# Attention with decay and a gated MLP on one core: four temporaries for the conversions of w_out, the first conversion ahead of the first MLP's second stage

## The chip, the cores and the metric

The kernel runs on one core of one Trainium2 chip. The metric is the device time of one execution in microseconds, lower is better. An execution under the hardware profiler gives the trace; its engines are called PE (TensorE, the matrix unit), DVE (VectorE), ACT (ScalarE), POOL (GpSimd) and SP (the queue that starts most transfers).

## The reference

The input is q, k, v for 8 batches, 8 heads, 576 tokens and head dimension 64, with a decay factor f per token. The attention's output, 512 wide, goes into a gated MLP:

```python
scores = scale * np.matmul(q, k.transpose(0, 1, 3, 2))
cum = np.cumsum(np.log(np.clip(f, 0.0001, 1.0)), axis=-1)
scores = np.where(causal, -1e9, scores + cum[:, :, :, None] - cum[:, :, None, :])
attn = softmax(scores);  x = heads_side_by_side(attn @ v)     # (8, 576, 512)
h = np.maximum(x @ w_in, 0.0)                                 # w_in: 512 x 1024
u, v = h[..., :512], h[..., 512:]
v_n = (v - mean(v)) / np.sqrt(var(v) + 1e-06)
v_s = einsum('ts,bsd->btd', w_spatial, v_n) + b_spatial[None, :, None]
return (u * v_s) @ w_out                                      # w_out: 512 x 512
```

Everything is float32.

## The kernel before

**Precision.** TensorE multiplies a rounded 32-bit type at full rate, so that each float32 operand is split into a rounded part (`hi`, tiles with an h or index 0) and the rest (`lo`, an l or index 1), and each product takes three matmuls. w_in and w_out come into the kernel as 64-bit floating-point words. `conv64` (L154) makes one 128-row part of such a matrix into the two 32-bit parts. For a part of 128 × 512 it issues nine operations: ACT takes the magnitude into a temporary called `wa` (L162); DVE runs L163, L165, L166, L168 and L169 (limit, shift and mask, join with the sign, exponent, scale of the low word), where L166 writes into the raw tile and L168 reads it; POOL adds (L171); ACT rounds to the high part (L172); POOL subtracts for the low part (L173). All read or write `wa`, so that a second conversion with the same temporary can begin only when L173 of the one before is done. The parts of w_out are `wo[0]` to `wo[3]`; in the listings they are `wo_` with a number.

**Attention.** `attention(b)` handles the batch's eight heads as four pairs P: scores (tiles `sc` from `ta` and `tb`), on DVE the maximum (L345), on ACT the exponential (L347), on POOL the scaling (L355; the last tokens' tile `tl` in L375 and L378), on TensorE the transposes (`tp`, L401), on ACT and DVE the split of these (`eh` L390, `el` L391), on TensorE the products with `vt`, and on ACT and DVE the split of their result (`xh` L449, `xl` L450). `lo` (L280) splits the next pair's q and k, `vt` (L322) its v, both on POOL.

**The MLP.** `moe(b)` has three stages. In the first, five blocks of `vx` = relu(x·w_in, second half) are normalised (L538 to L555) and split into `vnh` and `vnl`; the fifth block has 64 tokens and keeps both parts in one `vnh` tile (L553). In the second, eight `u` tiles come from the first half of w_in (L559 to L570). In the third, for the first 256 and then the other 320 tokens, four gate tiles are the products of `vnh`, `vnl` with w_spatial (`sph`, `spl`; for the fifth block `spta`) times u, split into `gh`, `gl` (L592, L593), and `w_out_tile` (L605) multiplies 128 of their tokens with the four parts of w_out. The last 64 tokens of two batches share one output tile; their gated parts are kept in the tile `gt`, which the even batch allocates. All of these sums go through two PSUM banks (pool `ps_m`, tile name `ps`), in turn.

**What sets the order.** Both are Python generators. The loop at the end advances attention of the next batch and the MLP of this one in shares of time (`LEAD`, `t_attn`, `t_moe`), and the tile framework's scheduler then orders each engine's instructions, by data, by free buffers and by the marks that `after` sets. A mark such as ("exp", 5, 1, 0) is an exponential of pair 5, head 1, tile 0. `load_late` is a third generator, which reads the late parts of the weights and converts them: it stops at each yielded mark and goes on as soon as attention has reached it (`converted`). At "m2" it waits for `open_m2`, which the first MLP calls ahead of its second stage; this closes the pool `wu` and opens `m2` in its place, for u, the gates, `gt` and the output tile `o`. The parts of w_out are converted after this, at the marks of four steps of pairs 5 and 6, all with the one temporary `o`, which the output tiles use too; the fourth part is read from memory at the first of these marks.

Of the kernel before, what the change touches and what calls it, by code (L numbers as in the profile page):

```python
# [9 lines left out]
F32R = mybir.dt.float32r  # L10
BF16 = mybir.dt.bfloat16
U32 = mybir.dt.uint32
# [14 lines left out]
DM = 512  # L27
# [6 lines left out]
def f32(ap):  # L34
    return ap.bitcast(F32)
# [3 lines left out]
def attn_gmlp_kernel(ctx: ExitStack, tc: tile.TileContext, qk, v, f, w_in, w_sp, b_sp, w_out, out):  # L39
# [9 lines left out]
    NJ = DM // 128  # L49
# [85 lines left out]
    win, wo, raws = {}, {}, {}  # L135
# [15 lines left out]
        raws[tag] = cst.tile([128, DM, 2], U32, name="w64", tag=tag)  # L151
        after(SY.dma_start(out=raws[tag], in_=src), mark)

    def conv64(tag, pool, behind, temp=None):  # L154

        raw = raws.pop(tag)
        lo, hi = raw[..., 0], raw[..., 1]
        a = pool.tile([128, DM], U32, name="wa", tag=temp or "wa")
        w = hi if temp else pool.tile([128, DM], U32, name="w32")[:]
        wf, af = w.bitcast(F32), a[:].bitcast(F32)  # L160

        after(A.activation(af, hi.bitcast(F32), AF.Abs), behind)  # L162
        V.tensor_scalar(out=af, in0=af, scalar1=2.0 ** -15, scalar2=None, op0=ALU.max)  # L163

        V.tensor_scalar(out=a, in0=a, scalar1=3, scalar2=0x3FFFFFF8, op0=ALU.logical_shift_left, op1=ALU.bitwise_and)  # L165
        V.scalar_tensor_tensor(out=w, in0=hi, scalar=0xC0000000, in1=a, op0=ALU.bitwise_and, op1=ALU.bitwise_or)  # L166

        V.tensor_scalar(out=a, in0=w, scalar1=0xFF800000, scalar2=None, op0=ALU.bitwise_and)  # L168
        V.scalar_tensor_tensor(out=af, in0=lo, scalar=2.0 ** -52, in1=af, op0=ALU.mult, op1=ALU.mult)  # L169
        t = cst.tile([128, 2, DM], F32R, name=tag, tag=tag)  # L170
        G.tensor_tensor(out=af, in0=wf, in1=af, op=ALU.add)  # L171
        A.copy(t[:, 0, :], af)  # L172
        G.tensor_tensor(out=t[:, 1, :], in0=af, in1=f32(t[:, 0, :]), op=ALU.subtract)  # L173
        return t
# [10 lines left out]
    def read_out(n, mark):  # L185
        read64(f"wo{n}", wo_v[:, n, :, :], mark)
# [44 lines left out]
    def load_late(wu):  # L231

        br = wu.tile([1, S], F32, name="br", bufs=1)
        bs = [wu.tile([1, S], F32R, name=f"bs{r}", bufs=1) for r in range(2)]
        SY.dma_start(out=br, in_=b_sp)
        yield ("exp", 5, 0, 0)
        read_out(1, ("exp", 5, 0, 0))
        read_out(2, ("exp", 5, 0, 0))
        unit(7, wu, ("exp", 5, 0, 0))
        A.copy(bs[0][:], br)  # L240
        V.tensor_tensor(out=bs[1][:], in0=br, in1=f32(bs[0][:]), op=ALU.subtract)
        for r in range(2):
            SY.dma_start(out=f32(sptb[64 + r:65 + r, :]), in_=f32(bs[r][:]))
        yield "m2"
        for n in range(NJ):
            m = ("exp",) + ((5, 1, 0), (6, 0, 0), (6, 0, 3), (6, 1, 0))[n]
            yield m
            if n == 0:
                read_out(3, m)
            wo[n] = conv64(f"wo{n}", m2[0], m, "o")  # L250
        yield None

    tl = cst.tile([128, 640], F32, name="tl")
# [249 lines left out]
    gt = {}  # L503
# [9 lines left out]
    def moe(b):  # L513
        X = [xs.pop(b * PPB + p) for p in range(PPB)]
        vh, vl = [], []
        for i in range(NB + 1):
            ps = acc(b)
            n = 0
            for p in range(PPB):
                xh, xl = X[p]  # L520
                if i < NB:
                    t = slice(128 * i, 128 * i + 128)
                    terms = ((xh[:, t], 0), (xh[:, t], 1), (xl[:, t], 0))
                else:
                    terms = ((xh[:, TL:640], 0), (xh[:, TL:640], 1))
                for l, r in terms:
                    mm(ps, l, win[p][:, r, :], n == 0, n == len(terms) * PPB - 1)
                    n += 1
                yield 648
            th = mo.tile([128, DM], F32R, name="vnh", tag="vnh", bufs=5)  # L530
            tlo = mo.tile([128, DM], F32R, name="vnl", tag="vnl", bufs=4) if i < NB else None
            x = mo.tile([128, DM], F32, name="vx", tag="vx", bufs=2)
            st = mo.tile([128, 6], F32, name="st", tag="st", bufs=2)
            mv = mo.tile([128, 2], F32, name="mv", tag="mv", bufs=2)
            m = slice(0, 128)
            if i == NB:
                m = slice(0, 64)
                A.copy(x[64:128, :], ps[64:128, :])  # L538
                V.tensor_tensor(out=x[m, :], in0=ps[m, :], in1=x[64:128, :], op=ALU.add)
            A.activation(x[m, :], ps if i < NB else x[m, :], AF.Relu)  # L540
            V.bn_stats(out=st[m, :], in_=x[m, :])
            V.bn_aggr(out=mv[m, :], in_=st[m, :])
            G.tensor_tensor(out=mv[m, 1:2], in0=mv[m, 1:2], in1=lnc[m, 0:1], op=ALU.add)
            G.tensor_tensor(out=mv[m, 1:2], in0=mv[m, 1:2], in1=lnc[m, 1:2], op=ALU.pow)
            V.tensor_scalar(out=x[m, :], in0=x[m, :], scalar1=mv[m, 0:1], scalar2=mv[m, 1:2],  # L545
                            op0=ALU.subtract, op1=ALU.mult)
            A.copy(th[m, :], x[m, :])
            if i < NB:
                G.tensor_tensor(out=tlo, in0=x, in1=f32(th[:]), op=ALU.subtract)
                vl.append(tlo)  # L550
            else:
                A.copy(vb_[m, :], x[m, :])
                G.tensor_tensor(out=th[64:128, :], in0=x[m, :], in1=f32(th[m, :]), op=ALU.subtract)  # L553
            vh.append(th)
            yield 0  # L555
        if b == 0:
            open_m2()
        us = {}
        for j in range(NJ):  # L559
            for t0, nt in HALVES:  # L560
                ps = acc(b)
                n = 0
                for p in range(PPB):
                    xh, xl = X[p]
                    for l, r in ((0, xh), (1, xh), (0, xl)):
                        mm(ps[:, 0:nt], win[NJ + j][:, l, 128 * p:128 * p + 128], r[:, t0:t0 + nt], n == 0, n == 3 * PPB - 1)
                        n += 1
                    yield 369
                us[j, t0] = m2[0].tile([128, 320], F32, name="u", tag="U", bufs=9)
                A.activation(us[j, t0][:, 0:nt], ps[:, 0:nt], AF.Relu)  # L570
        if b % 2 == 0:
            gt[0] = m2[0].tile([128, 2, NJ, 128], F32R, name="gt", tag="gt")
        r0 = 64 * (b % 2)
        for t0, nt in HALVES:
            gh, gl = [], []
            for j in range(NJ):
                ps = acc(b)
                o = ps[:, 0:nt]
                js = slice(128 * j, 128 * j + 128)
                for c in range(NB):  # L580
                    mm(o, vh[c][:, js], sph[c][:, t0:t0 + nt], c == 0, False)
                    mm(o, vh[c][:, js], spl[c][:, t0:t0 + nt], False, False)
                    mm(o, vl[c][:, js], sph[c][:, t0:t0 + nt], False, False)
                    yield 370
                mm(o, vh[NB][:, js], spta[:, t0:t0 + nt], False, False)
                mm(o, vb_[:, js], sptb[:, t0:t0 + nt], False, True)
                yield 246
                g = us[j, t0][:, 0:nt]
                V.tensor_tensor(out=g, in0=o, in1=g, op=ALU.mult)
                gh.append(m2[0].tile([128, 320], F32R, name="gh", tag="GH", bufs=3))  # L590
                gl.append(m2[0].tile([128, 320], F32R, name="gl", tag="U", bufs=9))
                A.copy(gh[j][:, 0:256], g[:, 0:256])  # L592
                G.tensor_tensor(out=gl[j][:, 0:256], in0=g[:, 0:256], in1=f32(gh[j][:, 0:256]), op=ALU.subtract)  # L593
                if t0:
                    th, tlo = (gt[0][:, r, j, r0:r0 + 64] for r in range(2))
                    A.copy(th, g[:, 256:320])
                    G.tensor_tensor(out=tlo, in0=g[:, 256:320], in1=f32(th), op=ALU.subtract)
            for c0 in (0, 128):
                yield from w_out_tile(b, [g[:, c0:c0 + 128] for g in gh], [g[:, c0:c0 + 128] for g in gl],
                                      [(b, t0 + c0, 0, 128)])  # L600
        if b % 2 == 1:
            yield from w_out_tile(b, *[[gt[0][:, r, j, :] for j in range(NJ)] for r in range(2)],
                                  [(b - 1, TL, 0, 64), (b, TL, 64, 64)])

    def w_out_tile(b, ghi, glo, dst):  # L605
# [25 lines left out]
    with tc.tile_pool(name="ws", bufs=2) as ws, tc.tile_pool(name="p0s", bufs=3, space=PSUM) as p0s, \  # L631
            tc.tile_pool(name="p0t", bufs=3, space=PSUM) as p0t:
        PS['s'], PS['t'] = p0s, p0t
        wgen = load_first(ws)
        need = next(wgen)
        for _ in attention(0, ws):
            while need in last:
                need = next(wgen, None)
# [7 lines left out]
    late, m2 = ExitStack(), []  # L646
    wgen = load_late(late.enter_context(tc.tile_pool(name="wu", bufs=1, reuse_waits="tile")))
    need = [next(wgen)]
# [66 lines left out]
```

## Time and profile before

| | us |
|---|---|
| median of 3 runs | 799.14 (799.07 to 799.27) |
| the profiled execution's own time | 797.53 |
| span of its trace | 795.7 |
| mean granted TensorE clock | 0.993 of full |
| PE busy | 778.9 (98%) |
| DVE busy | 556.6 (70%) |
| ACT busy | 534.9 (67%) |
| POOL busy | 476.4 (60%) |

All times in the trace are microseconds from the span's start. A row of the timeline gives the start, the duration, the engine, the line, the operation, the output tile <- the input tiles and the shapes, and in brackets how long the engine had idled and what ended that. A window gives each engine's busy time and number of instructions in a stretch, and the clock that TensorE was granted in it (1.00 is full). The program starts with attention alone; the first MLP runs from about 75 us, and the conversions of w_out lie between 107 and 164 us.

### The profile page before, as it was taken

What the parts mean: (1) busy time and instruction counts of PE and PEld (TensorE: products, weight loads), DVE (VectorE), ACT (ScalarE), POOL (GpSimd) and SP (SyncE); (2) the same over time, 40 slices, a digit from 0 to 9 for tenths busy, and PEclk for the clock granted to TensorE, in tenths of its full rate; (3) what the DMA queues carried; (4) which work ended last, traced back from release to release, by engine and by line L of the source; (5) the groups of instructions that cost most, each with busy time, mean ns of one, the idle gap of its engine ahead of it and who ended that gap; (6) DMA issues with size and microseconds to landing.
All of it is one profiled execution on the core that took longest, in us unless ns stands there. A gap on an engine that the chain in (4) does not pass through costs nothing.

```text
span 795.7 us, 15502 instructions
## 1 busy us (share of the span) xinstructions
PE 778.9 (98%) x4980; PEld 702.3 (88%) x4981; DVE 556.6 (70%) x1665; ACT 534.9 (67%) x1418; POOL 476.4 (60%) x660
## 2 busy tenths in 40 slices
PE   8999989899999999999999999999999999999997
PEld 4767779798999989998999989999899988998996
DVE  7889778975767667766866668766787658674421
ACT  7787678675777777667766668766686767764431
POOL 5777798664865647465655647554776537643251
PEclk9999999999999999999999999999999999999999
DMA  9967744566454565365454555564555465320001
GB/s 246 239 185 185 188 119 121 119 168 171 103 123 119 153 152 142 102 148 136 104 143 129 133 145 114 131 170 135 141 134 138 108 164 134 78 75 14 28 1 67
DMA packets 41713, 103.48 MB, mean 130 GB/s; under 512 B 6831, under 2 KB 8879, under 8 KB 41568
## 3 DMA queue, kind: packets, MB, share of 16 engines
q1 hardware_dynamic: 41306, 101.96, 49.7%
q8 instruction: 40, 0.66, 0.4%
q10 hardware_dynamic: 326, 0.53, 0.3%
q14 instruction: 41, 0.34, 0.1%
HBM read 39.42 MB, written 10.68 MB: 63 GB/s over the span
## 4 chain that ended last, share of the span: by engine, by line
PE 86%; DVE 6%; ACT 3%; POOL 2%; issue 2%; DMA 1%; ACTq 0%; POOLq 0%; DVEq 0%
PE ps L260 45%; PE sc L260 16%; PE x L260 12%; PE tp L401 8%; PE tp L260 2%; PE tp L414 2%; DVE tt L345 1%; POOL tt L355 1%; DVE el L391 1%; DVE xl L450 1%; DVE wa L163 0%; ACT eh L390 0%; DVE vx L545 0%; ACT tt L347 0%; ACT hi L278 0%
## 5 line engine op out<-in xcount | busy, mean ns | idle before, releaser
L355 POOL TENSOR_SCALAR tt<-tt,sm 128x128 f32<-128x128 f32 (+3 forms) x256 | 142.0, 573 | 74.9 <-DVE sm L351 56.4
L345 DVE CUSTOM_DVE_ANT_0 tt<-sc,zm 128x128 f32<-128x128 f32 (+3 forms) x256 | 122.8, 486 | 85.0 <-PE tp L401 63.4
L390 ACT CAST eh<-tp 128x512 fp32r<-128x512 f32 (+1 forms) x270 | 111.4, 426 | 75.4 <-PE tp L401 50.2
L347 ACT ACTIVATE tt<-tt,nm 128x128 f32<-128x128 f32 (+3 forms) x256 | 144.4, 565 | 23.7 <-DVE nm L345 21.9
L391 DVE TENSOR_TENSOR el<-tp,eh 128x512 fp32r<-128x512 f32 (+1 forms) x270 | 127.2, 485 | 26.2 <-ACT eh L390 23.8
L401 PE MATMUL tp<-ident,tt 128*128 128x128 f32 x640 | 111.6, 277 | 4.1 <-DVE el L391 4.1
L260 PE MATMUL sc<-ta 128*128 128x128 f32 (+1 forms) x336 | 109.1, 330 | 2.5 <-DVE nm L345 2.0
L260 PE MATMUL sc<-tb 68*128 68x128 f32 (+1 forms) x336 | 106.2, 320 | 0.0
L260 PE MATMUL x<-eh,vt 128*128 128x320 f32 (+4 forms) x378 | 102.5, 287 | 0.0
L593 POOL TENSOR_TENSOR gl<-u,gh 128x256 fp32r<-128x256 f32 x64 | 47.7, 745 | 87.7 <-ACT gh L592 78.1
L260 PE MATMUL ps<-xh,win 128*128 128x256 f32 (+1 forms) x464 | 99.3, 304 | 0.4 <-ACT u L570 0.3
L280 POOL TENSOR_TENSOR lo<-raw,hi 128x640 fp32r<-128x640 f32 (+1 forms) x56 | 84.2, 1525 | 16.1 <-ACT hi L278 15.9
L260 PE MATMUL ps<-win,xh 128*128 128x512 f32 x296 | 90.6, 396 | 0.0
L260 PE MATMUL x<-el,vt 128*128 128x256 f32 x324 | 90.1, 303 | 0.0
L401 PEld LDWEIGHTS tp<-ident,tt 128*128 128x128 f32 x640 | 76.3, 141 | 14.2 <-issue 2.7
L449 ACT CAST xh<-x 64x256 fp32r<-64x256 f32 (+1 forms) x128 | 49.8, 394 | 42.3 <-PE x L260 40.3
L260 PEld LDWEIGHTS ps<-xh,win 128*128 128x128 f32 x464 | 76.3, 192 | 2.0 <-ACT u L570 0.9
L260 PE MATMUL ps<-sph,vnh 128*128 128x256 f32 (+1 forms) x240 | 73.2, 305 | 0.4 <-ACT o L618 0.4
L260 PEld LDWEIGHTS x<-eh,vt 128*128 128x128 f32 x378 | 71.3, 190 | 2.5 <-POOL vt L322 0.3
L260 PE MATMUL ps<-wo,gh 128*128 128x512 f32 x224 | 71.9, 405 | 0.0
L260 PEld LDWEIGHTS sc<-ta 128*128 128x128 f32 x336 | 64.3, 191 | 8.6 <-DVE nm L345 4.5
L260 PE MATMUL ps<-sph,vnl 128*128 128x256 f32 (+1 forms) x240 | 71.6, 298 | 0.0
(178 smaller groups left out, 1916.4 us busy)
## 6 DMA issues: line engine op xcount, KB each, us to landing
raw<-in_dram SPq DMA_DIRECT2D x28, 608.0 KB
ta<-hi SPq DMA_DIRECT2D x56, 304.0 KB
vraw<-in_dram SPq DMA_DIRECT2D x32, 320.0 KB
tb<-hi SPq DMA_DIRECT2D x56, 160.0 KB
ta<-lo SPq DMA_DIRECT2D x56, 160.0 KB
out_dram<-o SPq DMA_DIRECT2D x32, 256.0 KB
ta<-hi SPq DMA_DIRECT2D x56, 144.0 KB
tb<-lo SPq DMA_DIRECT2D x56, 144.0 KB
```

What stands on the lines that cost most here:

```text
L260: last['mm'] = T.matmul(o, l, r, start=st, stop=sp)
L280: G.tensor_tensor(out=lo[:, c], in0=raw[:, c], in1=f32(hi[:, c]), op=ALU.subtract)
L345: V.tensor_tensor_reduce(out=t, in0=sc[:, 0:n], in1=zm[:, 640 - n:640], scale=-0.125, scalar=3.0e38, op0=ALU.add, op1=ALU.min, accum_out=n ...
L347: last["exp"] = last["exp", P, h, i] = A.activation(t, t, AF.Exp, bias=nm[:, i:i + 1], scale=-1.0, accum_out=se[:, i, 0:1])
L355: G.tensor_scalar(out=t, in0=t, scalar1=sm[:, i:i + 1], scalar2=1.0, op0=ALU.mult, op1=ALU.mult)
L390: A.copy(h_ap, ps)
L391: V.tensor_tensor(out=l_ap, in0=ps, in1=f32(h_ap), op=ALU.subtract)
L401: T.transpose(out=tp[:, (i - c) * 128:(i - c + 1) * 128], in_=tt[h][:, TOFF[i] + 128 * c:TOFF[i] + 128 * c + 128], identity=ident)
L414: T.transpose(out=tp[:, j * 128:(j + 1) * 128], in_=tl[:, c * 128:(c + 1) * 128], identity=ident)
L449: last[P, h] = A.copy(hi, ps[m0:m0 + 64, 0:n])
L450: V.tensor_tensor(out=lo, in0=ps[m0:m0 + 64, 0:n], in1=f32(hi), op=ALU.subtract)
L593: G.tensor_tensor(out=gl[j][:, 0:256], in0=g[:, 0:256], in1=f32(gh[j][:, 0:256]), op=ALU.subtract)
```

## The change

The four conversions no longer share one temporary. The first part is converted while the pool `wu` is still open, with that pool's temporary `wb` and ahead of "m2", at the mark ("exp", 5, 0, 2), and the read of the fourth part moves to this mark too. The second and third use the two buffers of a tag `gt`, the fourth uses `o`. The gate tile `gt`, until now one tile for both parts, becomes two tiles with the same tag, allocated when the second group of tokens begins; before that, the generator of conversions is run to its end. So all conversions stand in the program ahead of the first w_out tile that could want a buffer of theirs. The marks of the second to the fourth part are (5,1,0), (6,0,0) and (6,0,3). No operation is added or removed.

```diff
-    def conv64(tag, pool, behind, temp=None):
+    def conv64(tag, pool, behind, temp=None, bufs=None):
...
-        a = pool.tile([128, DM], U32, name="wa", tag=temp or "wa")
+        a = pool.tile([128, DM], U32, name="wa", tag=temp or "wa", bufs=bufs)
...
+        yield ("exp", 5, 0, 2)
+        read_out(3, ("exp", 5, 0, 2))
+        wo[0] = conv64("wo0", wu, ("exp", 5, 0, 2), "wb")
         yield "m2"
-        for n in range(NJ):
-            m = ("exp",) + ((5, 1, 0), (6, 0, 0), (6, 0, 3), (6, 1, 0))[n]
+        for n, m, tag, bufs in ((1, (5, 1, 0), "gt", 2), (2, (6, 0, 0), "gt", 2), (3, (6, 0, 3), "o", 1)):
+            m = ("exp",) + m
             yield m
-            if n == 0:
-                read_out(3, m)
-            wo[n] = conv64(f"wo{n}", m2[0], m, "o")
+            wo[n] = conv64(f"wo{n}", m2[0], m, tag, bufs)
         yield None
...
-        if b % 2 == 0:
-            gt[0] = m2[0].tile([128, 2, NJ, 128], F32R, name="gt", tag="gt")
         r0 = 64 * (b % 2)
         for t0, nt in HALVES:
+            if t0 and b % 2 == 0:
+                while need[0]:
+                    need[0] = next(wgen)
+                gt[0] = [m2[0].tile([128, NJ, 128], F32R, name="gt", tag="gt", bufs=2) for r in range(2)]
...
-                    th, tlo = (gt[0][:, r, j, r0:r0 + 64] for r in range(2))
+                    th, tlo = (gt[0][r][:, j, r0:r0 + 64] for r in range(2))
...
-            yield from w_out_tile(b, *[[gt[0][:, r, j, :] for j in range(NJ)] for r in range(2)],
+            yield from w_out_tile(b, *[[gt[0][r][:, j, :] for j in range(NJ)] for r in range(2)],
```

Lines from `load_late` on shift by one, from the gate stage on by three. What the scheduler makes of the change is seen in three places.

DVE, where the second part's conversion begins. A row is the line, the operation and out<-in; `w_1051`, `w_1053` and `w_1081` are the raw second, third and fourth part. Before:

```order
L163 TENSOR_SCALAR wa<-wa 128x512
L545 TENSOR_SCALAR vx<-vx,mv 64x512
L391 TENSOR_TENSOR el<-tp,eh 128x128
L165 TENSOR_SCALAR wa<-wa 128x512
L350 TENSOR_REDUCE sm<-se_108 128x4
L166 SCALAR_TENSOR_TENSOR w_1051<-w_1051,wa 128x512
L351 RECIPROCAL sm<-sm 128x4
L345 ISA tt_67,nm<-sc,zm 128x128
```

And now:

```order
L163 TENSOR_SCALAR wa<-wa 128x512
L546 TENSOR_SCALAR vx<-vx,mv 128x512
L163 TENSOR_SCALAR wa<-wa 128x512
L165 TENSOR_SCALAR wa<-wa 128x512
L163 TENSOR_SCALAR wa<-wa 128x512
L392 TENSOR_TENSOR el<-tp,eh 128x256
L392 TENSOR_TENSOR el<-tp,eh 128x128
L165 TENSOR_SCALAR wa<-wa 128x512
L166 SCALAR_TENSOR_TENSOR w_1051<-w_1051,wa 128x512
L165 TENSOR_SCALAR wa<-wa 128x512
```

Three conversions are interleaved from here on, fifteen operations in the 32 rows from the first L163 to the last L169, where one stood before; on ACT the three L162 stand in a row ahead of the first `u`.

POOL, around the `vnh` of the fifth block (64x512), which the first `spta` product on TensorE reads. Before:

```order
L173 TENSOR_TENSOR wo_1542<-wa,wo_1542 128x512
L378 TENSOR_SCALAR tl<-tl,sm 128x576
L544 TENSOR_TENSOR mv<-mv,lnc 64x1
L553 TENSOR_TENSOR vnh<-vx,vnh 64x512
L355 TENSOR_SCALAR tt_68<-tt_68,sm 128x128
```

And now, behind three L171 in a row:

```order
L544 TENSOR_TENSOR mv<-mv,lnc 64x1
L356 TENSOR_SCALAR tt_67<-tt_67,sm 128x128
L356 TENSOR_SCALAR tt_67<-tt_67,sm 128x256
L356 TENSOR_SCALAR tt_67<-tt_67,sm 128x384
L356 TENSOR_SCALAR tt_67<-tt_67,sm 128x512
L173 TENSOR_TENSOR wo_1553<-wa,wo_1553 128x512
L173 TENSOR_TENSOR wo_1564<-wa,wo_1564 128x512
L545 TENSOR_TENSOR mv<-mv,lnc 64x1
L173 TENSOR_TENSOR wo_1575<-wa,wo_1575 128x512
L376 TENSOR_SCALAR tl<-tl,sm 128x64
L379 TENSOR_SCALAR tl<-tl,sm 128x576
L554 TENSOR_TENSOR vnh<-vx,vnh 64x512
```

The conversions of the second, third and fourth part now stand ahead of `vnh`; before, the second's L171 was five rows behind it.

PE, in the first two w_out tiles, where the products with the third part begin. Before:

```order
L260 MATMUL ps<-wo_1553,gl 128x512
L260 MATMUL x_1880<-eh,vt 128x256
L260 MATMUL x_1880<-el,vt 128x256
L260 MATMUL x_1880<-eh,vt 128x128
L260 MATMUL x_1880<-el,vt 128x128
L260 MATMUL ps<-wo_1564,gh 128x512 x2
L260 MATMUL x_1881<-eh,vt 128x320
```

And now:

```order
L261 MATMUL ps<-wo_1553,gl 128x512
L261 MATMUL ps<-wo_1564,gh 128x512 x2
L261 MATMUL ps<-wo_1564,gl 128x512
L261 MATMUL ps<-wo_1090,gh 128x512 x2
L261 MATMUL ps<-wo_1090,gl 128x512
L261 MATMUL ps<-wo_1553,gh 128x512 x2
L261 MATMUL ps<-wo_1553,gl 128x512
L261 MATMUL ps<-wo_1564,gh 128x512 x2
```

The products with the first three parts now follow one another in both tiles, where attention stood between them. The first `spta` product on PE has 53 more matmuls ahead of it than before. Behind about 290 us of the old trace the orders of all engines are the same.

## The prediction

> **What bounds the kernel now.** I read the page's busy line first, then windows of the span by stage, then the rows inside the two windows that stand out.
>
> ```profile
> PE 778.9 (98%) x4980; PEld 702.3 (88%) x4981; DVE 556.6 (70%) x1665; ACT 534.9 (67%) x1418; POOL 476.4 (60%) x660
> ```
>
> TensorE (PE) is busy 98% of the span, so a change can win only what TensorE loses somewhere. The windows say where. Their columns are start and end, length, then busy time and count of PE, PE's weight loads, DVE, ACT and POOL, then the granted TensorE clock, the DMA share and GB/s.
>
> ```profile
> 100.00:120.00 20.00, 17.92 (x105) 15.62 (x104) 15.90 (x41) 15.17 (x37) 18.45 (x20) 0.91 0.50 124
> 120.00:140.00 20.00, 20.00 (x156) 19.77 (x155) 17.62 (x52) 16.84 (x45) 16.94 (x24) 1.00 0.48 123
> 140.00:160.00 20.00, 16.76 (x107) 14.27 (x105) 18.85 (x49) 12.92 (x34) 13.71 (x16) 0.90 0.51 121
> 180.00:340.00 160.00, 159.93 (x1070) 148.85 (x1069) 113.92 (x346) 111.64 (x298) 95.67 (x137) 1.00 0.53 134
> 108.00:112.00 4.00, 1.96 (x8) 1.15 (x9) 3.90 (x13) 4.00 (x10) 2.46 (x4) 0.98 0.00 0
> 112.00:116.00 4.00, 4.00 (x20) 4.00 (x19) 4.00 (x7) 2.63 (x8) 4.00 (x4) 0.60 0.18 35
> 153.00:159.00 6.00, 2.76 (x10) 1.13 (x8) 5.81 (x14) 4.19 (x10) 4.34 (x6) 0.77 0.06 10
> 159.00:163.00 4.00, 4.00 (x19) 3.98 (x19) 2.96 (x11) 2.60 (x9) 4.00 (x4) 0.50 0.30 91
> ```
>
> From 180 us on TensorE is full at full clock. There are two holes before that. In the first, it idles 2.04 us of 108 to 112 and then runs four microseconds at clock 0.60, which loses 1.6 more. That hole costs 3.64 us, with its fringes some 3.7. In the second, TensorE idles 3.24 us of 153 to 159, runs the other 2.76 at 0.77 (0.6 lost), and then four microseconds at 0.50 (2.0): 5.9 us, or 6.65 if the whole 1.4 us by which the clock falls short in 153 to 159 fell on matmuls. I take 6.3. Together 10 us: no version can win more than that here.
>
> The second hole is the one that the four w_out conversions make. TensorE's timeline:
>
> ```profile
> 153.28 0.40 PE L260 MATMUL ps<-wo,gl 128*128 128x512 f32 x1
> 154.70 0.44 PE L260 MATMUL sc<-ta 128*128 128x384 f32 x1 [1.03 <-DVE nm L345]
> 159.00 0.45 PE L401 MATMUL tp<-ident,tt 128*128 128x128 f32 x1 [1.81 <-DVE el L391]
> 162.94 0.51 PE L260 MATMUL ps<-wo,gh 128*128 128x512 f32 x1
> ```
>
> Between 153.28 and 162.94 no piece of a w_out tile runs: both open tiles (the pool has two banks) wait for the third converted part and later for the fourth. TensorE has only attention left, and attention goes through DVE, which in 140 to 160 is busy 18.85 of 20. What DVE does in the hole is the conversion itself; the chain of waits runs through it:
>
> ```profile
> 156.56 1.70 DVE wa L169
> 158.30 0.57 DVE el L391
> ```
>
> **The change, part by part.** No operation is added or removed; 36 conversion operations (nine a part) change place, and the temporaries no longer queue them one behind the other.
>
> *What it takes away.* In the new order wo1, wo2 and wo3 are converted together, before the gate stage, and the products of the w_out tiles stand almost without a gap on TensorE. Nothing of a conversion is left behind 146 us or so. The second hole goes: −6.3 us (−5.9 to −6.65).
>
> *What it adds.* The same operations now stand ahead of something else. POOL runs in order, and in the new order all three L171 and all three L173 stand ahead of the last block's `vnh` (L553 before), which in the old order stood ahead of them. The first gate tile's `spta` product on TensorE waits for that `vnh`, and everything behind it on TensorE waits too. In the trace it came here:
>
> ```profile
> 0.00:133.06 133.06, 126.36 (x674) 98.01 (x676) 112.09 (x335) 99.93 (x257) 100.40 (x130) 0.99 0.71 187
> 0.00:139.70 139.70, 133.00 (x727) 104.55 (x729) 118.34 (x352) 106.03 (x272) 107.04 (x137) 0.99 0.69 183
> 128.08 1.33 POOL L553 TENSOR_TENSOR vnh<-vx,vnh 64x512 fp32r<-64x512 f32 x1 [2.96 <-ACT vnh L547]
> ```
>
> The first `spta` product began at 133.06, with 674 matmuls before it. The new order has 53 more ahead of it, most of them attention's; 727 matmuls had been run by 139.70. So the new `spta` is on a par with the old kernel if it comes at 139.70, and each microsecond later is one lost. When does `vnh` end?
>
> First, where DVE's burst begins. It stands behind the maxima of one attention head, which ended at 126.2:
>
> ```profile
> 101.34 0.69 DVE L541 BATCH_NORM_STATS2 st<-vx 128x6 f32<-128x512 f32 x1 [2.35 <-ACT vx L540]
> 118.12 0.68 DVE L539 TENSOR_TENSOR vx<-ps,vx 64x512 f32<-64x512 f32 x1
> 126.13 0.08 DVE L345 DVE_READ_ACCUMULATOR2_ANT nm<- 128x1 f32 x1
> ```
>
> Taken from before it are wo0's five operations (4.68, next fence; they move up to where DVE idled, as for 2.35 us at 101) and the last block's L539, L541 and L542 (0.68, 0.69 and a short one, 1.5). That is 120.0, less what DVE idles in between while TensorE falls behind less, some 1.8 us: 118.2. I take 118.2, with 117.5 and 120 as ends.
>
> Second, what a conversion costs DVE. All instructions on the temporaries (min/median/max ns), then DVE's time in the four w_out conversions (columns DVE, ACT, POOL):
>
> ```profile
> L163 DVE TENSOR_SCALAR wa<-wa x12: 418/570/1305, 16.7 to 151.5; 128x512 f32<-128x512 f32 x12
> L165 DVE TENSOR_SCALAR wa<-wa x12: 403/506/931, 17.2 to 152.0; 128x512 uint32<-128x512 uint32 x12
> L166 DVE SCALAR_TENSOR_TENSOR w<-w,wa x12: 672/694/1951, 17.7 to 153.1; 128x512 uint32<-128x512 uint32 x12
> L168 DVE TENSOR_SCALAR wa<-w x12: 404/425/1408, 18.8 to 154.6; 128x512 uint32<-128x512 uint32 x12
> L169 DVE SCALAR_TENSOR_TENSOR wa<-w,wa x12: 658/712/1700, 19.6 to 156.6; 128x512 f32<-128x512 uint32 x12
> L171 POOL TENSOR_TENSOR wa<-w,wa x12: 1266/1292/1436, 22.2 to 158.4; 128x512 f32<-128x512 f32 x12
> 108.60:116.20 7.60, 4.68 (x5) 0.00 (x0) 0.00 (x0) 0.78 0.12 28
> 126.00:130.50 4.50, 3.27 (x5) 0.00 (x0) 0.00 (x0) 1.00 0.96 209
> 138.50:147.00 8.50, 4.32 (x5) 0.00 (x0) 0.00 (x0) 1.00 0.71 184
> 151.50:158.30 6.80, 3.82 (x5) 0.00 (x0) 0.00 (x0) 0.84 0.05 13
> ```
>
> The shortest five add up to 2.56 us, the medians to 2.91, the four w_out conversions took 3.27 to 4.68. What stretches them shows in one pair: the L169 of 156.56 took 1.70, and it began inside this POOL operation, which ended at 157.71:
>
> ```profile
> 156.16 1.55 POOL L322 TENSOR_TENSOR vt<-vraw,vt 128x640 fp32r<-128x640 f32 x1
> ```
>
> 1.15 us of waiting and 0.66 of work make 1.81, near the 1.70. POOL will be busy nearly throughout the burst, but half its operations there are the short scalings; I take 3.8 each, below the mean of the four (4.02), with 2.9 and 4.7 as ends. The Trainium skill has a rule for this: its GPSIMD Engine Reference, Key points, says that GpSimd shares its SBUF interfaces with VectorE and contends with VectorE operations that have two SBUF inputs or a two-port mode. By that page alone, with L166 and L169 each meeting half an L171-long operation, a conversion would be an estimated 2.56 + 2 × 0.65 = 3.9 us and the forecast 0.2 us later, which the pair above agrees with.
>
> Third, what lies among and behind the conversions:
>
> ```profile
> L355 POOL TENSOR_SCALAR tt<-tt,sm 128x128 f32<-128x128 f32 (+3 forms) x256 | 142.0, 573 | 74.9 <-DVE sm L351 56.4
> L345 DVE CUSTOM_DVE_ANT_0 tt<-sc,zm 128x128 f32<-128x128 f32 (+3 forms) x256 | 122.8, 486 | 85.0 <-PE tp L401 63.4
> L391 DVE TENSOR_TENSOR el<-tp,eh 128x512 fp32r<-128x512 f32 (+1 forms) x270 | 127.2, 485 | 26.2 <-ACT eh L390 23.8
> L280 POOL TENSOR_TENSOR lo<-raw,hi 128x640 fp32r<-128x640 f32 (+1 forms) x56 | 84.2, 1525 | 16.1 <-ACT hi L278 15.9
> 145.67 0.75 POOL L378 TENSOR_SCALAR tl<-tl,sm 128x576 f32<-128x576 f32 x1
> 115.58 2.01 POOL L322 TENSOR_TENSOR vt<-vraw,vt 128x640 fp32r<-128x640 f32 x1
> ```
>
> On DVE the burst's other operations are four L345 (0.49 each), four L391 (0.49), three on `vx` (about 0.53) and small ones of 0.8 together: 6.3 us. The burst ends at 118.2 + 6.3 + 3 × 3.8 = 135.9. Then POOL has the last L171 (1.3), four scalings (2.3), three L173 (1.3 each, as L171), tl (1.1), mv (0.7) and `vnh` (1.33): 10.6 us, so 146.5. POOL by itself would need 25.8 us after the `vt` above (12.6 before the first L171: eight scalings 4.6, two vnl 2.6, two lo 3.05, tl 1.1, mv 1.3; then three L171 3.9 and the last 9.3); that `vt` ended at 117.6 and comes 0 to 1.3 later, since wo0's two operations (2.6) go ahead of it and one vnl (1.3) behind: 143.8 with 118.0, which is the floor. DVE decides: 146.5, `spta` at 146.6, 6.9 us behind par: +6.9 us, first hole included, since the par row has it too.
>
> *Costed at nothing.* wo0's conversion moves up into 90 to 103, where DVE has idle slots such as the 2.35; without that cover it is 4.7 us of DVE. read_out(3) goes one step earlier on SP's queue; 0.52 MB at the 248 GB/s that 124 GB/s at share 0.50 stand for is 2.1 us, and DMA moves nothing in 108 to 112, so no load behind it is missed; uncovered it delays the next head's loads by 2.1. Three L162 stand ahead of the first u activation on ACT (2.0 us); TensorE is waiting for `vnh` in that stretch anyway, else it is 2.0. The gate tile in two pieces moves no operation.
>
> *Sum.* +6.9 − 6.3 + 0.2 (a rest of reduced clock once TensorE is fed again, between 0 and the first hole's 1.6) = +0.8 us on the profiled execution's 797.53 (span 795.7): 798.3. The median of the runs lies 1.61 above that execution: 799.9.
>
> **Rivals.** The whole rests on p, DVE's price of a conversion in the burst: the difference is 3 × (p − 3.8) + 0.8. What a measurement of this kernel tells from no change is about 0.2%, 1.6 us; faster by that needs p under 3.0, slower over 4.1.
>
> *A, faster.* The operations run near their medians, 2.9, because POOL stands still while DVE works. For it: wo1 took 3.27 beside an idle POOL. Against it: POOL has 12.6 us of other work exactly then. POOL's floor of 143.8 decides: 143.9 is 4.2 behind par, +4.2 − 6.3 + 0.2 = −1.9, 797.2; with `vt` at 117.6, the scalings 0.7 shorter, the hole at 6.65 and no rest 795.6.
>
> *B, slower.* The burst stretches itself: POOL's L171 and splits block DVE as the lo, vnl and vt of 110 to 117 did, p is wo0's 4.68, `vnh` ends at 149.1 and TensorE waits: +9.5 − 6.3 + 0.2 = +3.4, 802.5; with the burst from 119.2 on, 803.5. It decides from p = 4.1. For it: two of the four were above that. Against it: the other two. The page named above speaks for it as well.
>
> *C, the change doesn't do what it says.* DVE is behind after the burst, attention is late again in the gate stage, and a hole as large as the first opens there: 0.8 + 3.7 = +4.5, 803.6. For it: DVE at 17.62 of 20 even where TensorE is full. Against it: 8.1 us of conversions (4.32 + 3.82) leave DVE there.
>
> **How the numbers follow.** No change 0.37, A 0.31, B 0.28, C 0.04. So faster 0.31, same 0.37, slower 0.32; the time is 799.9, its own range 797.5 to 800.8 (p from 3.0 to 4.1). For 8 in 10 the range takes in A's and B's ends: 795.5 to 803.5.
>
> **What would show it.** Right: no hole in 150 to 165, w_out products in one run, first `spta` near 146.6 behind `vnh`, fifteen conversion operations on DVE between 118 and 136 with about 11.4 us in all, a lower clock around 111 to 118. Wrong: `spta` before 143.8 (A and more), after 148 (B), TensorE idle behind `spta` (C), or a difference that arises behind 290 us, where both orders are the same.

## The result

The changed kernel takes 804.54 us (median of 4 runs, 803.73 to 806.34) against 799.2 for the kernel before: the ratio is 1.0069, with a 95% interval of 1.0051 to 1.0086. A second set of runs (e10, below) gave 803.23 against 798.2, 1.0064 (1.0049 to 1.0079). The change is slower by 5 to 5.5 us. I had forecast 799.9, no difference that could be told from none, with a range of 795.5 to 803.5: the time lies above the range.

The page of the changed kernel's profiled execution (804.38 us, clock 0.992):

```profile
span 802.6 us, 15512 instructions
PE 781.9 (97%) x4981; PEld 703.1 (88%) x4981; DVE 557.9 (70%) x1665; ACT 535.1 (67%) x1418; POOL 474.3 (59%) x660
```

All engines but TensorE are busy for as long as before, to within 2.1 us, so the same work is done; TensorE has 3.0 us more busy time and 3.9 us more idle time in a span that is 6.9 us longer. The windows by stage, with the columns of the prediction:

```profile
100.00:120.00 20.00, 16.62 (x88) 12.36 (x87) 16.44 (x49) 16.21 (x42) 20.00 (x28) 0.93 0.63 155
120.00:140.00 20.00, 17.49 (x122) 16.31 (x122) 18.92 (x42) 12.66 (x34) 15.20 (x17) 0.98 0.42 110
140.00:160.00 20.00, 18.57 (x119) 17.22 (x119) 14.08 (x39) 11.93 (x33) 12.26 (x15) 0.83 0.31 72
144.00:148.00 4.00, 2.81 (x18) 2.08 (x17) 2.99 (x7) 2.61 (x5) 3.82 (x5) 1.00 0.01 2
148.00:152.00 4.00, 3.77 (x16) 3.23 (x16) 3.74 (x11) 3.43 (x13) 2.42 (x3) 0.51 0.23 65
152.00:156.00 4.00, 4.00 (x22) 3.92 (x21) 2.15 (x6) 1.41 (x5) 0.77 (x2) 0.63 0.04 17
160.00:180.00 20.00, 20.00 (x133) 18.63 (x132) 13.59 (x41) 13.45 (x37) 11.88 (x17) 1.00 0.56 154
```

The old second hole, 153 to 163, is gone. In its place TensorE idles 3.38, 2.51 and 1.43 us in the three windows from 100 to 160, and its clock is 0.51 and 0.63 over 148 to 156. DVE's fullest window has moved from 140 to 160 to the one before.

The first `spta` product on TensorE, and the POOL rows ahead of it:

```profile
148.21 0.58 PE L261 MATMUL ps<-spta,vnh 128*128 128x256 f32 x1 [0.50 <-POOL vnh L554]
134.29 4.74 POOL L171 TENSOR_TENSOR wa<-w,wa 128x512 f32<-128x512 f32 x3
143.70 0.54 POOL L545 TENSOR_TENSOR mv<-mv,lnc 64x1 f32<-64x1 f32 x1
146.89 1.27 POOL L554 TENSOR_TENSOR vnh<-vx,vnh 64x512 fp32r<-64x512 f32 x1
```

And the chain of waits that ends there:

```profile
134.34 3.72 POOL wa L171 x3
139.17 2.03 POOL tt L356 x4
141.20 0.84 POOL wo L173
142.44 1.29 POOL wo L173
143.73 0.52 POOL mv L545
144.25 0.03 issue
144.27 0.90 DVE vx L546
146.89 1.28 POOL vnh L554
```

The fifth block's `mv` had its statistics from DVE at 137.9; its second POOL step ran at 143.7, behind three L171, four scalings and two L173, and `vnh` behind a third L173. From 128.5 until `vnh` ends POOL is busy, with no gap over 0.1 us.

To compare kernels whose orders differ, I weight each matmul record of a trace with the columns that it streams and compare the starts of matmuls at equal sums (the trace of the kernel before lacks one record of 512 columns at 15 us, which is added). The next table is worked out in this way from one profiled execution each, averaged over 2 us, in microseconds later (+) or earlier (−) than the kernel before; the last column is the difference of the spans. e8 has the old order row for row, so it is the kernel before once more: it differs from it by 1.1 us, and so do the two executions of the changed kernel from each other. About a unit is the limit of what the table tells. The experiments of its rows follow below.

| kernel | at before's 121 | at 138 | at 150 | at 186 | at the end |
|---|---|---|---|---|---|
| changed | +3.4 | +6.6 | +12.5 | +4.9 | +6.9 |
| changed, again (e10) | +5.4 | +6.8 | +11.5 | +3.9 | +5.5 |
| e1: first part early, one temporary | +4.0 | +4.0 | +4.7 | −0.5 | +2.9 |
| e2: separate temporaries, first part not early | +6.1 | +8.9 | +8.8 | +1.1 | +8.9 |
| e3: changed, POOL's part behind `vnh` | +3.4 | +7.0 | +7.5 | +0.7 | +3.9 |
| e4: changed, parts 2 to 4 left out | +3.9 | +4.2 | +4.0 | −2.9 | 0.0 |
| e5: before, parts 2 to 4 left out | −0.1 | 0.0 | 0.0 | −7.0 | −4.7 |
| e6: third part with a temporary of its own | +1.4 | +1.8 | +8.7 | +1.4 | +7.3 |
| e7: fourth part with a temporary of its own | −0.1 | +1.6 | +3.1 | −4.2 | +1.8 |
| e8: before, another LEAD, the same order | +1.1 | +1.1 | +1.1 | +1.1 | +1.6 |
| e9: changed, first part later, still in wu | +7.2 | +13.0 | +12.8 | +5.7 | +7.9 |

Between 150 and 186 every row but e8's falls by 5 to 8 us: this is where the kernel before has its second hole. So the changed kernel got the hole back, 7.6 us of it, but was 12.5 us behind when it came there, and lost 2.0 us more later.

### The profile page after: what moved, and what is told of

Read it like the earlier page. It is cut to its first block, busy times and chain, and to the rows that moved or that the text cites. A ratio compares the mean times of both kernels' runs of the same rounds, so it can differ in the third digit from the quotient of the medians.

```text
span 802.6 us, 15512 instructions
## 1 busy us (share of the span) xinstructions
PE 781.9 (97%) x4981; PEld 703.1 (88%) x4981; DVE 557.9 (70%) x1665; ACT 535.1 (67%) x1418; POOL 474.3 (59%) x660
## 4 chain that ended last, share of the span: by engine, by line
PE 84%; DVE 4%; ACT 3%; DMA 3%; POOL 3%; issue 2%; SPq 1%; ACTq 0%; POOLq 0%; DVEq 0%
PE ps L261 44%; PE sc L261 16%; PE x L261 12%; PE tp L402 8%; PE tp L261 2%; PE tp L415 2%; DMA out_dram<-o 1%; DVE tt L346 1%; POOL tt L356 1%; DMA w<-in_dram 1%; ACT hi L279 1%; ACT eh L391 1%; DMA tb<-hi 1%; DVE vx L546 1%; DVE el L392 0%
## 5 line engine op out<-in xcount | busy, mean ns | idle before, releaser
L356 POOL TENSOR_SCALAR tt<-tt,sm 128x128 f32<-128x128 f32 (+3 forms) x256 | 139.7, 565 | 79.5 <-DVE sm L352 62.2
L261 PE MATMUL x<-el,vt 128*128 128x256 f32 x324 | 91.7, 307 | 0.0
L451 DVE TENSOR_TENSOR xl<-x,xh 64x256 fp32r<-64x256 f32 (+1 forms) x128 | 57.4, 451 | 20.8 <-ACT xh L450 18.2
```

Of the source, the lines that this page charges most:

```text
L261: last['mm'] = T.matmul(o, l, r, start=st, stop=sp)
L356: G.tensor_scalar(out=t, in0=t, scalar1=sm[:, i:i + 1], scalar2=1.0, op0=ALU.mult, op1=ALU.mult)
L451: V.tensor_tensor(out=lo, in0=ps[m0:m0 + 64, 0:n], in1=f32(hi), op=ALU.subtract)
```

## The experiments

**e1: the early first part alone.** The first part is converted early in wu and the fourth is read early; the others keep the one temporary.

```diff
         yield "m2"
-        for n in range(NJ):
-            m = ("exp",) + ((5, 1, 0), (6, 0, 0), (6, 0, 3), (6, 1, 0))[n]
+        for n in range(1, NJ):
+            m = ("exp",) + ((5, 1, 0), (6, 0, 0), (6, 0, 3))[n - 1]
             yield m
-            if n == 0:
-                read_out(3, m)
             wo[n] = conv64(f"wo{n}", m2[0], m, "o")
```

(ahead of "m2" stand the three lines of the change.)

> One half of the change alone: the first part of w_out is converted early in the pool wu and the fourth part is read early; the other three parts keep the one temporary o, one after the other, and the gate tile stays whole. Theory T (three conversions bunched ahead of the fifth block's vnh keep DVE and POOL from attention and from vnh): only the second part's two POOL operations (2.6 us) stand ahead of vnh, the first spta product moves from 148.2 back to about 143, TensorE waits less for it and the clock loss behind it shrinks: 797.5 to 801. Rival W (the second stage waits for the pool swap, which now waits for the first part's last operation, at 115 in the changed kernel): that wait is kept whole, so 802.5 to 806, near the changed kernel's 804.5.

Measured: 800.61 us, ratio 1.0029 (1.0015 to 1.0042). The total is T's. But W is not refuted by it: in the table e1 is 4.0 to 4.7 us late from 121 to 150, and the first u activation comes at 118.87, nearly where the changed kernel has it. What e1 does not have is the second step, from +6.6 to +12.5. The three conversions one after another cost 2.4 us at 186 (−0.5 against e4's −2.9), in the changed kernel's bunch 7.8 (+4.9 against −2.9).

**e2: the separate temporaries alone.** All four parts behind the swap at their old marks, with the temporaries o, gt, gt, o.

```diff
+        for n, m, tag, bufs in ((0, (5, 1, 0), "o", 1), (1, (6, 0, 0), "gt", 2), (2, (6, 0, 3), "gt", 2), (3, (6, 1, 0), "o", 1)):
```

> The other half alone: all four parts stay behind the pool swap at their old marks, but have separate temporaries (o, two of gt, o again), with the gate tile in two pieces. Theory T: four conversions follow each other closely from 107 us on, seven of their eight POOL operations stand ahead of vnh, and DVE has some ten more operations (about 8 us) ahead of the first spta product than before the change; the second hole goes (-6), spta is about 6 to 9 late: 799 to 804. Rival W (the pool swap): the pool is given up at the old time, the second stage begins as before, the hole goes without a price: 794 to 797.5.

Measured: 806.16 us, 1.0101 (1.0084 to 1.0118), slower than the changed kernel itself and above both expectations. At 138 it is 8.9 us late, as T had it; at 186 it is only 1.1 late, and the other 7.8 us are lost behind that. W's range is far off. But the total doesn't show that bunching alone costs as much as the change does: up to 186, it costs no more than the table's unit.

**e3: POOL's part behind `vnh`.** L171 and L173 of parts 2 to 4 are ordered behind the fifth block's `vnh` on POOL; DVE's order in the burst stays.

```diff
-        G.tensor_tensor(out=af, in0=wf, in1=af, op=ALU.add)
+        add = G.tensor_tensor(out=af, in0=wf, in1=af, op=ALU.add)
+        if tag in ("wo1", "wo2", "wo3"):
+            after(add, "vnh4")
```

(the same for L173; `last["vnh4"]` is the fifth block's `vnh`.)

> The changed kernel, with one more rule of order: L171 and L173 of the second, third and fourth part go behind the fifth block's vnh on POOL. DVE's order in the burst is the same as in the changed kernel. Theory T, POOL's part: the six operations (7.8 us) no longer stand ahead of mv and vnh; vnh ends at about 142 instead of 148.2, TensorE idles some 5 us less and w_out does not wait, since its first tile runs at 172 only: 797.5 to 801. If DVE's part of T decides (the statistics of the fifth block come behind DVE's burst, at 137): vnh at 145 or later, 801.5 to 804. Rival W (pool swap): no difference, 803.5 to 806.

Measured: 801.1 us, 1.0032 (1.0021 to 1.0044): between T's range and the one for DVE's part. About 3 us of the change's 5 to 5.5 are gone, and at 186 4.2 of its 4.9. The timelines of TensorE and of POOL:

```profile
144.34 0.36 PE L265 MATMUL ps<-spta,vnh 128*128 128x256 f32 x1
137.96 0.18 POOL L548 TENSOR_TENSOR mv<-mv,lnc 64x1 f32<-64x1 f32 x1 [3.65 <-DVE sm L356]
139.47 0.54 POOL L549 TENSOR_TENSOR mv<-mv,lnc 64x1 f32<-64x1 f32 x1
141.77 1.28 POOL L558 TENSOR_TENSOR vnh<-vx,vnh 64x512 fp32r<-64x512 f32 x1 [1.08 <-ACT vnh L552]
143.13 3.85 POOL L171 TENSOR_TENSOR wa<-w,wa 128x512 f32<-128x512 f32 x3
```

`mv` now has its second step 1.5 us behind its first instead of 4.7, `vnh` ends at 143.1 instead of 148.2, and `spta` runs at 144.3. The place of these six operations in POOL's queue is worth about 4 of the 7.8 us of the bunch. No run isolates the other 3.6 (+0.7 against e4's −2.9 at 186); DVE is the likely cause, since POOL now waits 3.65 us for DVE just ahead of `mv`.

**e4: the changed kernel with the conversions of parts 2 to 4 left out.**

```diff
-            wo[n] = conv64(f"wo{n}", m2[0], m, tag, bufs)
+            wo[n] = wo[0]
```

> The changed kernel with the conversions of the second, third and fourth part left out altogether: their place in the products is taken by the first part, so the output is not the reference's. It takes 12.3 us off DVE and 7.8 us off POOL and leaves the pool swap as it is. Theory T: vnh is some 10 us earlier, neither hole is left, 790 to 795. Rival W: the second stage still waits for the swap; at least half of the loss stays, 799 or more.

Measured: 798.25 us, 0.9998 (0.9985 to 1.0011). Neither expectation: with three of four conversions gone the kernel is no faster than before. It is late by about 4 us from 121 to 150, without a bunch that could cause it; at 186 it is 2.9 us ahead, and it loses that again behind 186. This was the result that made the early first part a suspect of its own.

**e5: the kernel before with the same conversions left out.**

```diff
-            wo[n] = conv64(f"wo{n}", m2[0], m, "o")
+            wo[n] = conv64(f"wo{n}", m2[0], m, "o") if n == 0 else wo[0]
```

> The kernel before with the conversions of the second, third and fourth part left out (the first part takes their place, so the output is not the reference's). Beside e4_left_out it shows what the early first part and the later pool swap cost by themselves. Theory W2 (the swap holds the second stage back and e4's 3.8 us of lateness at equal work around 146 us is its price): here equal work around 146 us comes at the old time (0 to +1) and around 186 us some 6 to 7 us earlier; 793 to 796 in all. Rival (the lateness in e4 is not the swap's): the same +3 to +4 and -3.4 as in e4, 797.5 to 799.

Measured: 793.62 us, 0.9936 (0.9918 to 0.9954): W2's range. There is no lateness here. Its windows beside those of e4, first e5's and then e4's:

```profile
100.00:120.00 20.00, 17.94 (x106) 15.65 (x105) 16.00 (x41) 15.17 (x37) 18.42 (x21) 0.91 0.51 125
120.00:140.00 20.00, 20.00 (x156) 19.78 (x155) 15.22 (x50) 16.38 (x45) 15.01 (x22) 1.00 0.51 131
140.00:160.00 20.00, 19.94 (x136) 18.53 (x135) 14.14 (x44) 13.64 (x39) 11.30 (x16) 1.00 0.52 131
```

```profile
100.00:120.00 20.00, 16.42 (x88) 12.27 (x87) 16.59 (x49) 15.61 (x42) 20.00 (x28) 0.97 0.63 156
120.00:140.00 20.00, 19.29 (x139) 18.85 (x139) 10.11 (x34) 12.88 (x32) 13.60 (x19) 0.94 0.52 132
140.00:160.00 20.00, 20.00 (x140) 18.45 (x139) 13.89 (x39) 12.54 (x33) 7.77 (x10) 1.00 0.27 65
```

In 100 to 140, e4 runs 227 matmuls and e5 262, with the same conversions left out of both. e5 shows two things more. The three conversions cost 7.0 us in the kernel before (its second hole and what hangs on it). And the early first part with what it entails costs 4.1 us at 186 (−2.9 against −7.0), 4.7 us in the spans (795.7 against 791.0), as long as the other three are left out.

**e6 and e7: one temporary more, in the kernel before.** In e6 the third part has a buffer of gt, in e7 the fourth; the others share o, and all stay behind the swap.

```diff
+        # e6
+        ... in ((0, (5, 1, 0), "o", 1), (1, (6, 0, 0), "o", 1), (2, (6, 0, 3), "gt", 2), (3, (6, 1, 0), "o", 1)):
+        # e7
+        ... in ((0, (5, 1, 0), "o", 1), (1, (6, 0, 0), "o", 1), (2, (6, 0, 3), "o", 1), (3, (6, 1, 0), "gt", 2)):
```

> The kernel before with one more temporary: the third part uses one buffer of gt (gate tile in two pieces), the others share o. All stay behind the pool swap. The conversions then stand apart from each other on DVE and POOL and end about 10 us earlier than before, and vnh keeps its place on POOL behind two conversions. Theory T (bunching ahead of vnh, not the earlier end, is what costs): no more than 2 us late around 146, 3 to 6 us early around 186, 794 to 798.5 in all. Rival D (each DVE operation moved ahead of the gate stage costs there what it wins later): 799 to 803.

> As e6, but it is the fourth part that has the temporary of its own; the order converts it second, with L171 ahead of vnh and L173 behind. One conversion less stands ahead of vnh than in e6's order. Theory T: as e6 or a little better around 146, the third part ends last, 794 to 798.5. Rival D: 799 to 803.

Measured: e6 804.83 us, 1.0061 (1.004 to 1.0082); e7 801.73, 1.0037 (1.0022 to 1.0053). T's totals are missed by both. e6 is 1.8 us late at 138, as T said, but then loses 7 us between 138 and 150: TensorE waits for DVE there,

```profile
145.39 0.61 PE L260 MATMUL sc<-ta 128*128 128x288 f32 x1 [3.41 <-DVE nm L345]
145.00:150.00 5.00, 3.74 (x15) 3.40 (x16) 4.81 (x15) 2.10 (x6) 0.73 (x1) 0.50 0.56 138
```

with DVE busy 4.81 of 5 us and the clock at 0.50: the hole has only moved forward. Part of its price is the clock: three of e6's nine runs, with a mean clock of 0.995 to 0.998, took 799.9 to 801.6 us, the other six, at 0.991 to 0.993, 804.5 to 805.7. e7 has the front that T wanted, 4.2 us early at 186, and loses 6 us behind it; its profiled execution, 799.25, is the fastest of its ten. Rival D's range holds e7's total, not its front; e6 lies above it.

**e8: another LEAD from the second batch on.**

```diff
-            while da < min(B, b + 1 + LEAD + dm):
+            while da < min(B, b + 1 + (0.27 if b else LEAD) + dm):
```

> The kernel before with LEAD 0.27 in place of 0.25 from the second batch on; the order of all engines is the old one up to about 200 us and another one behind it, no conversion moves. Theory O (the old order behind 186 us is a favourable one, and every edit that shuffles it loses 2 to 5 us there, which is where 2.3 us of the change went): 801 to 804. Rival (the losses behind 186 us are an after-effect of moved conversions): 798 to 800.

Measured: 798.5 us, 0.9997 (0.9986 to 1.0007). The run tells nothing on theory O. The edit's premise was wrong: the order of all engines is the old one, row for row, but for the numbers of buffers. What it gives is a second profiled execution of the old order, the e8 row of the table.

**e9: the first part later, in wu as before.** In the changed kernel, wo0's first DVE operation is ordered behind the third block's normalisation.

```diff
+        if tag == "wo0":
+            held.append(lim)
...
+            if b == 0 and i == 2:
+                last["norm"] = norm
+                for k in held:
+                    after(k, "norm")
```

(`lim` is L163, `norm` the normalisation of `vx` on DVE.)

> The changed kernel, with wo0's first DVE operation (and with it its conversion) ordered behind the third block's normalisation; it keeps its temporary in wu, so the pool swap now waits for a later conversion. In the order the first u activation comes yet later on ACT (17 rows behind the changed kernel's place). Theory W (the second stage is tied to the pool swap, and this is worth the 3.8 us between e4 and e5): the second stage begins later still, 805 to 810. Rival N (the 3.8 us come from wo0's DVE operations standing ahead of the first stage's normalisation at 92 to 99 us): that is undone here, 798.5 to 802.

> The changed kernel once more, for the comparison with e9 and the others on a chip of their day: 1.005 to 1.009 of the kernel before by either theory.

Measured: e9 804.98 us, 1.0081 (1.006 to 1.0102), and e10, the changed kernel beside it, 803.23. N falls. W's total is met but for 0.02 us. The first u activation on ACT, in the kernel before, the changed one and e9, in this order:

```profile
111.61 0.39 ACT L570 ACTIVATE u<-ps 128x256 f32<-128x256 f32 x1
```

```profile
119.38 0.38 ACT L571 ACTIVATE u<-ps 128x256 f32<-128x256 f32 x1
```

```profile
132.81 0.37 ACT L580 ACTIVATE u<-ps 128x256 f32<-128x256 f32 x1
```

The later wo0 is done, the later u begins. In the five other kernels without the early first part (e2 and e5 to e8) this row comes at 111.5 to 113.4, in the other four with it (e1, e3, e4, e10) at 117.7 to 120.8. e9 is 13 us late at 138, but at 186 only 0.8 later than the changed kernel (1.8 later than e10), so its total does not show what a late u costs. No row shows ACT waiting for a POOL operation in front of these three: on the chip it is the position in ACT's order that holds u. That the scheduler gives it this position because wu closes later, and not by some other effect of the early conversion on the order, is likely but not shown: no run has the early conversion with a temporary outside wu.

**What the runs add up to.** With the prices at 186 us: e5 stands 7.0 us ahead of the kernel before. The early first part takes 4.1 of it, the bunch of three takes 7.8, so the changed kernel is 4.9 behind; 2.0 more come later. The kernel before paid 7.0 for the same three conversions, one after the other in its own place. These prices hold in this order of adding alone: at 186 the early first part by itself (e1) costs −0.5 us and the separate temporaries by themselves (e2) 1.1, both within the table's unit, and only the two together cost 4.9. The gate tile in two pieces was never tried by itself.

Behind 186, all variants lose something, e2 most (7.8 us). Compared row by row, the kernels fall in two groups there. e8 has the order of the kernel before throughout, e1 again from about 221 us and the changed kernel from about 377; from 350 on these lose at most 0.5 us against it. The other seven (e2 to e7 and e9) keep another order to the end of the program, the same one in all of them from about 556, and lose 2.0 to 4.3 us from 350 on, in short waits that the kernel before doesn't have. So 2 us or more of their totals go with the order far behind the edit. No run changes that order alone. In the changed kernel the loss lies between 240 and 350; its two largest waits of 262 to 350 come first, then one that stands in each of the seven and in none of the others, here in e5 (total us, times, longest us):

```profile
PE ps L261 <- ACT o L621: 0.7, 1, 0.7
PE sc L261 <- DVE nm L346: 0.5, 1, 0.5
PE x L260 <- POOL vt L322: 0.9, 1, 0.9
```

No version faster than the kernel before came out of it; of those that move a conversion and do all the work, e1 is the nearest.

## Why the prediction was wrong

**What bounds the kernel: right.** Two holes worth some 10 us together, and nothing to win beyond them. e5 puts the second at 7.0 with what hangs on it (I took 6.3).

**"The second hole goes": right.** 7.6 us of lateness are recovered between 150 and 186.

**The place: right. "DVE decides": wrong.** `spta` waits for `vnh`, behind all of the conversions on POOL, and e3 shows what that queue is worth. The forecast was 146.6, measured were 148.2 and, in e10, 149.2. The burst on DVE, first in the changed kernel's first execution (three rows), then in e10:

```profile
119.80 0.42 DVE L163 TENSOR_SCALAR wa<-wa 128x512 f32<-128x512 f32 x1
135.89 0.70 DVE L169 SCALAR_TENSOR_TENSOR wa<-w,wa 128x512 f32<-128x512 uint32 x1
119.80:136.59 16.79, 11.79 (x15) 0.00 (x0) 2.29 (x2) 0.97 0.33 87
121.13:135.00 13.87, 8.84 (x15) 0.00 (x0) 0.00 (x0) 0.92 0.32 79
```

It begins at 119.8 (forecast 118.2) and ends at 136.6 (135.9); the fifteen operations take 11.79 us, 3.93 a part (3.8). I had said that the whole rests on this price p. But in e10 they take 8.84 us, 2.95 a part, which by my rule would have made the kernel faster, and `spta` comes a microsecond later. That the price and the place came out near my forecast in the first execution was luck: in both executions POOL decides. It runs from `lo` into the three L171 without a wait for DVE, and on to `vnh`. My floor for POOL, 143.8, counted its operations from the end of `vt` (116.6 in the trace, 118.0 in e10) and no waits; the operations came out about 1 us longer than I took, and POOL waited 4.8 us (4.3 in e10) on the way:

```profile
122.08 1.30 POOL L550 TENSOR_TENSOR vnl<-vx,vnh 128x512 fp32r<-128x512 f32 x1 [1.24 <-ACT vnh L548]
125.86 1.54 POOL L550 TENSOR_TENSOR vnl<-vx,vnh 128x512 fp32r<-128x512 f32 x1 [2.48 <-ACT vnh L548]
128.48 2.75 POOL L356 TENSOR_SCALAR tt<-tt,sm 128x128 f32<-128x128 f32 x4 [1.08 <-DVE sm L352]
136.26 3.83 POOL L171 TENSOR_TENSOR wa<-w,wa 128x512 f32<-128x512 f32 x3
```

The last row is e10's: its L171 begin 1.3 us behind the end of DVE's burst. The first two waits are for `vnh` tiles that ACT rounds as soon as DVE has normalised `vx`, at 121.1 and 125.1, among the first operations of the burst. So DVE enters by where the burst begins and by what stands in it early, not by where it ends. `spta` behind 148 was my sign for rival B. B's place came true, but not its cause, a price of 4.68 a part.

**"Costed at nothing": the step that failed first.** wo0's conversion was to lie in DVE's idle slots of 90 to 103. The slot of 2.35 us that I quoted lay at 99 to 101, and the operations came at 91.7 to 101.6, four of the five ahead of the second of two normalisations (98.1 and 99.0; 95.8 and 96.7 before) and of `vnl` (103.0; 99.4). I had looked at DVE alone. That the second stage would begin 7.8 us later (119.4 for 111.6) wasn't in the working at all. The two kernels without the other conversions put the term at 4.1 us (e4 against e5 at 186; 4.7 in the spans) in place of nothing. My price without cover, 4.7 us, is near that by chance: it was DVE's time, and e9, which takes wo0's operations away from those normalisations, gains nothing.

**"0.2, a rest of reduced clock": the term that was furthest off.** Between `spta` (8.5 us behind par) and the equal work of 150 (12.5) lie 4.0 us more, against 0.2. In the first profiled execution it is the clock, 0.51 and 0.63 over eight microseconds after TensorE had starved; TensorE idles only 0.23 of these eight. In the second, the clock stayed at 1.00, and the same stretch cost 2.0 us (9.5 at `spta`, 11.5 at 150); most of TensorE's idle time there lies ahead of `spta`, which is at 149.2:

```profile
144.00:148.00 4.00, 2.31 (x18) 1.95 (x16) 2.55 (x5) 1.62 (x3) 3.82 (x6) 1.00 0.02 6
148.00:152.00 4.00, 2.83 (x15) 1.80 (x15) 3.31 (x10) 3.70 (x11) 2.73 (x2) 1.00 0.05 7
```

Rival C had a loss in this stretch, with 803.6 us the nearest of the four numbers, and I had given it a chance of 0.04. Its number came near, not its cause: C had attention late and TensorE idle behind `spta`. In the working I had set the clock's price at 0.2 between ends of 0 and 1.6, while the first hole had already shown 1.6. The Trainium skill, in TensorE: Matmul & The Clock Gate, What's actually happening, calls the window by which the clock is judged free-running and its effect variable from run to run. These two executions of one program agree with that: 1.19 us idle in 144 to 148 and then 0.51 here, 1.69 idle and then 1.00 there.

**What was not in the sum.** 2.0 us behind 186. I had taken the orders to be the same behind about 290 us; row by row they differ in places up to about 372 us on TensorE and 376 on DVE.

**In sum:** +0.8 forecast; +1.6 for the later `spta` (8.5 for 6.9), +3.8 for the stretch behind it, −1.3 for a hole that was worth 7.6 instead of 6.3, +2.0 for what came later: +6.9, the difference of the spans. For e10 the same terms are +2.6, +1.8, −1.3 and +1.6: +5.5. The medians differ by 5.3 us, less than the first sum, since the profiled execution of the kernel before was 1.6 us faster than its median; I had added these 1.6 to the forecast, and the changed kernel's own profiled execution is 0.2 from its median.

## What to carry to other kernels

More buffers let work move; they don't hide it. Taking a serialisation off three conversions let them stand together ahead of an instruction on an in-order queue, and 7.0 us of waiting became 7.8, which is no gain. When a forecast hangs on which of two engines decides, put the waits for other engines into both sums: POOL's sum without its waits gave 143.8; it waited 4.8 us, and `vnh` ended at 148.2. When an operation moves ahead of the opening of a pool, look for what is ordered behind it, and look for the moved operation's neighbours on every engine that it uses, not only on the one with idle slots. And a starved matrix engine can cost more than the wait: what comes behind the wait ran at a low clock in one execution and not in the other, so a forecast needs a row for that stretch, taken from a hole that the trace already shows. Last, an edit can change the scheduler's order far behind its place: compare kernels at equal work just behind the edit as well as by their totals.

## What the runs showed of the hardware

Where the clock falls is not fixed by the program: in the changed kernel's two profiled executions the mean of 140 to 160 us was 0.83 and 1.00, of 120 to 140 0.98 and 0.92, and the spans differ by 1.4 us. The kernel before and e8, with one order, had 0.60 and 0.50 in 112 to 116, and e8 is 1.1 us later from there on.

DVE operations with one input can stretch beside POOL as much as those with two: in the burst an L168, which takes 0.41 us alone, took 1.63, beside a `lo` on POOL; in the kernel before, an L166, with two inputs, took 1.95 for 0.67.

```profile
131.41 1.63 DVE L168 TENSOR_SCALAR wa<-w 128x512 uint32<-128x512 uint32 x1
131.20 3.14 POOL L281 TENSOR_TENSOR lo<-raw,hi 128x640 fp32r<-128x640 f32 x2
```
